# w_phi loaded behind the first v rows, k folds in a row, later output projection steps, in a gated attention and FFN kernel

## The chip, the cores and the metric

One core of one Trainium2 chip runs the whole kernel. The metric is device time in microseconds (us), the median over several executions. Stage times come from one profiled execution of each kernel; there time is counted from the beginning of the span, which is about 1.3 us shorter than the device time. PE is TensorE's matmul pipe, PEld its weight loads, DVE the vector engine, ACT the scalar engine, POOL and SP the other two, and ACTq and SPq the queues on which ACT and SP issue DMAs.

## The reference, cut to what matters

```python
x = A_x                                           # 1 x 2048 x 640, bf16
g = sigmoid((x * gate_w).sum(-1, keepdims=True))
q, k, v = split(x @ wqkv)                         # 32 heads of 20
pq, pk = q @ w_phi, k @ w_phi                     # per head, 20 x 20
phi = lambda p: concat([softmax(p), softmax(-p)]) # for q and k
kv = phi(pk).T @ v ; z = sum(phi(pk))
a = ((phi(pq) @ kv) / (phi(pq) @ z + 1e-6)) @ wo
b = (gelu(x @ w_gate) * (x @ w_up)) @ w_down
return g * a + (1 - g) * b
```

The kernel folds w_phi into the k and q weights once (the "folds": weights times a block diagonal BD made from w_phi), so that it gets pk and pq straight from x.

## The kernel before

First the loads; SP's are issued in this order.

```python
xload("sp", 0); xload("sp", 2)                  # x rows of tiles 0,1 and 2,3; PE transposes them
sc.dma("act", ... wphi_sb <- w_phi ..., reads=["ident"], writes=["wphi"])   # 640 pieces of 40 B
for kt in range(KD):                            # v's weight rows, five loads of 160 KB
    sc.dma("sp", ... w3[:, kt, 0:D] <- wqkv[kt, 2*D:3*D] ..., writes=[("wv", kt)])
sc.dma("act", ... gz <- gate_w ...)
xturn(4, 2)                # x rows of tiles 4,5, transposed by the DMA
wload(self.wkT, D, "wkT")  # k weights, transposed by the DMA
xturn(6, 2)                # x rows of tiles 6,7
wload(self.wqT, 0, "wqT")  # q weights
xturn(8, 4); xturn(12, 4)
... # FFN weights, wo; masks made on POOL
```

Then the start of the attention state. `xt` transposes x on PE, `vs(t, kt)` is one step of v of tile t, `v_early(t, bank)` all of v of a tile, `f(kt, "k"/"q", banks, engine)` a fold with its evacuation to SBUF by DVE ("d") or ACT ("a"), `k_early` the keys of a tile, `pq` a query block, `gram` the update of kv.

```python
for n in (512, 512, 512, 512, 512, 512, 128):   # matmuls of a constant, before x is there
    ... matmul(bank 0, ones, ones)
xt(0, 6, "d"); xt(1, 7, "a"); xt(2, 2, "d"); xt(3, 3, "d")
for t in range(4): vs(t, 0)                     # and so for kt = 1, 2, 3
self.blockdiag()                                # DVE: BD from w_phi and the masks
self.gate_column(6)
... # vs(t, 4) and evacuations
self.v_early(4, 6)
self.v_early(5, 0)
f(0, "k", (2, 3), "d")
f(1, "k", (4, 5), "a")
self.v_early(6, 6)          # needs x of tiles 6,7
f(2, "k", (2, 3), "d")
f(3, "k", (4, 5), "a")
f(4, "k", (0, 1), "d")
self.v_early(7, 6)
self.k_early(0, 2)
f(0, "q", (4, 5), "d")      # needs wqT
f(1, "q", (6, 7), "d")
self.k_early(1, 0)
... # f 2 q, f 3 q, keys 2, f 4 q
self.k_norm(0)              # DVE: sums of the keys' exponentials, reciprocal, scaling
self.k_early(3, 0)
self.k_norm(1)
self.pq(0, 1, 1); self.pq(0, 0, 0); self.pq(0, 3, 3, 0)
self.gram(0)
```

And the order of the output steps of a pair of tiles:

```python
for q in range(2 * nw):
    h, opens = q % nw, q < nw                   # h: a stretch of output columns
    cs = list(range(NFC + 1 if opens else NFC)) + [NFC + 1 + k for k in range(KD)]  # FFN, then wo steps
    for x, c in enumerate(cs): ... # two row halves of PE
```

The softmax here doesn't subtract the row's maximum and nothing guards it: scores larger than these inputs give would overflow.

Of the kernel before, what the change touches and what calls it, by code (L numbers as in the profile page):

```python
# [3 lines left out]
P = 128  # L4
# [103 lines left out]
class _Kernel:  # L108
    S, D, H, DH, F = 2048, 640, 32, 20, 1728
    KD = D // P  # L110
# [4 lines left out]
    NFC = 14  # L115
# [92 lines left out]
    def loads(self):  # L208
        sc, nc = self.sc, self.nc
        D, KD, DH, P_ = self.D, self.KD, self.DH, P  # L210
        w3 = self.wqkv.rearrange("(kt p) n -> p kt n", p=P)

        x4 = self.x[0:self.BT, :].rearrange("(p j) n -> p j n", j=self.TB)

        def xload(q, j):
            sc.dma(q, lambda e: e.dma_start(self.xtok[:, j:j + 2, :], x4[:, j:j + 2, :]),  # L216
                   writes=[("xtok", j), ("xtok", j + 1)])

        def wload(T, c0, key):
            sc.dma("sp", lambda e: e.dma_start_transpose(T[:, :, :], self.wqkv[:, c0:c0 + D]), writes=[key])  # L220

        def xturn(t, n):
            a, z = t * P, (t + n) * P
            sc.dma("sp", lambda e: e.dma_start_transpose(self.xT[:, :, a:z], self.x[a:z, :]),
                   writes=[("xT", k) for k in range(t, t + n)])
        sc.op("pool", lambda e: e.memset(self.gz[:, :], 0.0), writes=["gz"])
        sc.op("act", lambda e: e.activation(self.gtmp[:, 0:1], self.nc.const_aps.tensor(1.0, [P, 1], BF16), AF.Exp),
              writes=["gtmp"])
        sc.op("pool", lambda e: e.memset(self.ident[:, :], 0.0), writes=["ident"])
        sc.op("pool", lambda e: e.affine_select(self.ident[:, :], self.ident[:, :], pattern=[[-1, P]],  # L230
                                                compare_op=ALU.not_equal, fill=1.0, base=0, channel_multiplier=1),
              writes=["ident"])
        xload("sp", 0)
        xload("sp", 2)
        sc.dma("act", lambda e: e.dma_start(
            self.wphi_sb[:, :, :], self.wphi.rearrange("h d f -> (h d) f").rearrange("(i p) f -> p i f", p=P)),
            reads=["ident"], writes=["wphi"])
        for kt in range(KD):
            sc.dma("sp", lambda e: e.dma_start(self.w3[:, kt, 0:D], w3[:, kt, 2 * D:3 * D]), writes=[("wv", kt)])
        sc.dma("act", lambda e: e.dma_start(self.gz[0:KD, :], self.gw.rearrange("(k p) -> k p", p=P)), writes=["gz"])  # L240
        xturn(4, 2)
        wload(self.wkT, D, "wkT")
        xturn(6, 2)
        wload(self.wqT, 0, "wqT")
        xturn(8, 4)
        xturn(12, 4)
        half = 7 * P
        g3 = self.wg.rearrange("(kt p) n -> p kt n", p=P)
        u3 = self.wu.rearrange("(kt p) n -> p kt n", p=P)
        for i, (a, b) in enumerate(((0, half), (half, 13 * P))):  # L250
            sc.dma("sp", lambda e, a=a, b=b: e.dma_start(self.wg_sb[:, :, a:b], g3[:, :, a:b]), writes=[("wg", i)])
            sc.dma("sp", lambda e, a=a, b=b: e.dma_start(self.wu_sb[:, :, a:b], u3[:, :, a:b]), writes=[("wu", i)])
            if i == 0:
                sc.dma("sp", lambda e: e.dma_start(self.wgu_sb[:, :, 0:64], g3[:, :, 13 * P:self.F]), writes=["wgu0"])
                sc.dma("sp", lambda e: e.dma_start(self.wgu_sb[:, :, 64:128], u3[:, :, 13 * P:self.F]), writes=["wgu1"])
        sc.dma("sp", lambda e: e.dma_start(self.wd_sb[:, 0:13, :],
                                           self.wd[0:13 * P, :].rearrange("(c p) n -> p c n", p=P)), writes=["wd"])
        for r in (0, 1):
            sc.dma("sp", lambda e: e.dma_start(self.wd_sb[64 * r:64 * r + 64, 13, :], self.wd[13 * P:self.F, :]),
                   writes=[("wd13", r)])  # L260
        sc.dma("sp", lambda e: e.dma_start(self.wo_sb[:, :, :], self.wo.rearrange("(kt p) n -> p kt n", p=P)),
               writes=["wo"])

        def pool(fn, writes, reads=()):
            sc.op("pool", fn, reads=reads, writes=writes)
        for i in range(KD):
            n = self.HHI[i] - self.HLO[i] + 1
            base = P * i - DH * self.HLO[i]
            m = self.mask[:, i, 0:n]
            pool(lambda e, m=m: e.memset(m, 1.0), [("mask", i)])  # L270
            pool(lambda e, m=m, n=n, base=base: e.affine_select(
                m, m, pattern=[[-DH, n]], compare_op=ALU.is_ge, fill=0.0, base=base, channel_multiplier=1),
                [("mask", i)])
            pool(lambda e, m=m, n=n, base=base: e.affine_select(
                m, m, pattern=[[DH, n]], compare_op=ALU.is_ge, fill=0.0, base=DH - 1 - base, channel_multiplier=-1),
                [("mask", i)])
        for r in (0, 1):
            m = self.hmask[:, r, :, :]
            pool(lambda e, m=m: e.memset(m, 1.0), [("hmask", r)])
            pool(lambda e, m=m, r=r: e.affine_select(  # L280
                m, m, pattern=[[4, KD], [-DH, self.HB]], compare_op=ALU.is_ge, fill=0.0, base=-64 * r,
                channel_multiplier=1), [("hmask", r)])
            pool(lambda e, m=m, r=r: e.affine_select(
                m, m, pattern=[[-4, KD], [DH, self.HB]], compare_op=ALU.is_ge, fill=0.0, base=DH - 1 + 64 * r,
                channel_multiplier=-1), [("hmask", r)])
        for s in range(self.NSV):
            pool(lambda e, s=s: e.memset(self.vaug[:, s, :, DH:self.DA], 1.0), [("vone", s)])
# [133 lines left out]
            reads=[("ps", b0 + 1)], writes=[("gcol", t)])  # L421

    def k_norm(self, t):
        sc = self.sc
        se = t % self.NSE
        H, DH = self.H, self.DH
        sc.op("dve", lambda e: e.tensor_reduce(  # L427
            self.Dk[:, se, 0, :].rearrange("p (s h) -> p s h", h=H),
            self.Ek[:, se, :, :].rearrange("p s (h d) -> p s h d", d=DH), AX.X, ALU.add),
            reads=[("Ek", se, 0), ("Ek", se, 1)], writes=[("Dk", se)])  # L430
        sc.op("dve", lambda e: e.reciprocal(self.Dk[:, se, 1, :], self.Dk[:, se, 0, :]),
              reads=[("Dk", se)], writes=[("Rk", se)])
        for s in (0, 1):
            v = self.Ek[:, se, s, :].rearrange("p (h d) -> p h d", d=DH)
            r = self.Dk[:, se, 1, s * H:(s + 1) * H].unsqueeze(2).to_broadcast([P, H, DH])
            sc.op("dve", lambda e, v=v, r=r: e.tensor_tensor(v, v, r, ALU.mult),  # L436
                  reads=[("Rk", se)], writes=[("Ek", se, s)])
# [97 lines left out]
    def attention_state(self):  # L535
        NT = self.NT
        order = [(b, i) for b in range(self.NB) for i in range(self.KD)]
        sc = self.sc
        ones = self.nc.const_aps.tensor(1.0, [P, 512], BF16)
        for n in (512, 512, 512, 512, 512, 512, 128):  # L540
            sc.op("pe", lambda e: e.matmul(self.bank(0, n), ones[:, 0:P], ones[:, 0:n], start=True, stop=True),
                  writes=[("ps", 0)])
        vs, ve, xt = self.v_step, self.v_first_evac, self.x_transpose
# [18 lines left out]
                ve([0, 1, 2], "a", True)  # L562
        ve([3], "d", True)
        f = self.fold
        self.v_early(4, 6)
        self.v_early(5, 0)
        f(0, "k", (2, 3), "d")
        f(1, "k", (4, 5), "a")
        self.v_early(6, 6)
        f(2, "k", (2, 3), "d")  # L570
        f(3, "k", (4, 5), "a")
        f(4, "k", (0, 1), "d")
        self.v_early(7, 6)
        self.k_early(0, 2)
        f(0, "q", (4, 5), "d")
        f(1, "q", (6, 7), "d")
        self.k_early(1, 0)
        f(2, "q", (4, 5), "d")
        f(3, "q", (6, 7), "d")
        self.k_early(2, 2)  # L580
        f(4, "q", (4, 5), "d")
        self.k_norm(0)
        self.k_early(3, 0)
        self.k_norm(1)
        self.pq(0, 1, 1)
        self.pq(0, 0, 0)
        self.pq(0, 3, 3, 0)
        self.columns = True
        self.gram(0)
        self.k_norm(2)  # L590
# [101 lines left out]
    def down_pair(self, t0, banks, widths):  # L692

        sc = self.sc
        ts = (t0, t0 + 1)
        NFC, KD = self.NFC - 1, self.KD
        nw = len(widths)
# [39 lines left out]
            sc.dma("sp", lambda e: e.dma_start(rows[:, :, c0:c1], self.outsb[:, os_:os_ + 2, c0:c1]),  # L737
                   reads=[("outsb", os_ + j, k) for j in (0, 1) for k in hs], writes=[("out", t0, h)])

        for q in range(2 * nw):  # L740
            h, opens = q % nw, q < nw
            cs = list(range(NFC + 1 if opens else NFC)) + [NFC + 1 + k for k in range(KD)]
            for x, c in enumerate(cs):
                for r in (0, 1):
                    mm(r, r if opens else 1 - r, h, c, opens, x, len(cs))
                if x == len(cs) - 1 and not opens:
                    evac(h)
                yield None

# [94 lines left out]
```

## Time and profile before

| | before |
|---|---|
| device time, median of 3 | 288.31 us (287.94 to 288.32) |
| span of the profiled run | 287.0 us |
| PE busy | 280.9 us, 98% |
| first v step starts | 6.36 us |
| first k fold starts | 14.59 us |
| gram 0 starts | 29.52 us |
| start of the last matmul, last landing | 283.84 and 287.00 us |

From the page of the kernel before: the span, busy times, granted clock by fortieths of the span, and the chain that ended last by engine and by line. L354 is the common projection and gate/up helper.

```profile
span 287.0 us, 7005 instructions
...
PE 280.9 (98%) x3017; PEld 185.7 (65%) x3032; DVE 174.9 (61%) x353; ACT 104.5 (36%) x199; POOL 5.3 (2%) x36
...
PEclk9999999999999999999999999999999999999999
...
PE 96%; DMA 2%; issue 1%; SPq 0%; ACT 0%
PE ps L354 61%; PE ps L713 28%; PE ps L657 2%; PE ps L366 2%; PE ps L452 2%; DMA w<-in_A_wqkv_dram 2%; PE ps L334 1%; SPq L216 0%; ACT outsb L726 0%; PE ps L316 0%
```

PE is busy 98% of the span, and 96% of the last chain is PE. So only PE's idle time or its slow stretches can be won. The waits of PE alone show one in the middle of work (columns: line, what it waited for, total us, times, longest us):

```profile
engine line waited for: us in total, times, longest us
PE ps L366 <- DMA w<-in_A_wqkv_dram: 1.1, 1, 1.1
PE ps L541 <- PEq L829: 0.8, 1, 0.8
```

The timeline of PE gives the moments (start us, us, engine, line, operation, out<-in, shapes, count, and in brackets the idle time before and what ended it):

```profile
3.72 1.53 PE L293 MATMUL ps<-ident,xtok 128*128 128x128 bf16 x20
6.36 4.53 PE L366 MATMUL ps<-w,xT 128*128 128x480 bf16 x32 [1.11 <-DMA w<-in_A_wqkv_dram]
...
14.59 0.79 PE L334 MATMUL ps<-BD,wkT 128*128 128x140 bf16 x12
15.33 1.53 PE L354 MATMUL ps<-w,xT 128*128 128x512 bf16 x10
16.70 1.11 PE L334 MATMUL ps<-BD,wkT 128*128 128x140 bf16 x18
```

The 20 transposes of x (L293) end near 5.25 us. The v steps (L366) then wait 1.11 us for the v weights. After two k folds (L334, 12 matmuls, start 14.59), v 6 starts at 15.33. No wait is noted there, but the trace's record of landings has the x rows of tiles 6 and 7 complete at 15.29 us. Two lines of the same timeline show w_phi's issue, and the block diagonals that need it:

```profile
1.69 0.47 ACTq L235 DMA_DIRECT2D wphi_sb<-in_A_w_phi_dram  x1
...
7.50 1.19 DVE L307 TENSOR_TENSOR BD<-wphi_sb,mask 128x140 bf16<-128x140 bf16 x5 [1.60 <-DMA wphi_sb<-in_A_w_phi_dram]
```

### The profile page before, as it was taken

How to read it: one execution, taken by the hardware profiler on the slowest of the kernel's cores; microseconds unless marked ns; L12 is line 12 of the kernel's file. 1: busy time of each engine (PE TensorE's matmuls, PEld its weight loads, DVE VectorE, ACT ScalarE, POOL GpSimd, SP SyncE). 2: the span in 40 equal slices, each digit the busy share in tenths (PEclk: the TensorE clock that was granted, in tenths of full speed). 3: DMA queues.
4: the chain of work that ended last, by engine and by line, in shares of the span. 5: the costliest groups of instructions: out<-in, count | busy, mean ns of one | idle time of the engine just before them, and what ended most of it. 6: DMA issues, size and time to landing. Idle time of an engine off the chain costs nothing.

```text
span 287.0 us, 7005 instructions
## 1 busy us (share of the span) xinstructions
PE 280.9 (98%) x3017; PEld 185.7 (65%) x3032; DVE 174.9 (61%) x353; ACT 104.5 (36%) x199; POOL 5.3 (2%) x36
## 2 busy tenths in 40 slices
PE   7999999999999999999999999999999999999995
PEld 3576689999994444444444444445777777777785
DVE  1348999999977553567242334225883883883801
ACT  3357887677653222322323223321112112112111
POOL 7000000000000000000000000000000000000000
PEclk9999999999999999999999999999999999999999
DMA  8999996000002000011000000000232343342121
GB/s 224 203 174 248 366 366 192 0 2 2 2 0 48 0 0 0 3 24 23 2 0 0 0 2 0 0 2 0 26 87 74 29 48 99 43 60 82 49 72 48
DMA packets 36937, 18.67 MB, mean 65 GB/s; under 512 B 28970, under 2 KB 36394, under 8 KB 36906
## 3 DMA queue, kind: packets, MB, share of 16 engines
q1 hardware_dynamic: 36240, 18.19, 26.8%
q8 instruction: 24, 0.39, 0.6%
q10 hardware_dynamic: 666, 0.03, 0.2%
q14 instruction: 7, 0.06, 0.1%
HBM read 9.04 MB, written 2.62 MB: 41 GB/s over the span
## 4 chain that ended last, share of the span: by engine, by line
PE 96%; DMA 2%; issue 1%; SPq 0%; ACT 0%
PE ps L354 61%; PE ps L713 28%; PE ps L657 2%; PE ps L366 2%; PE ps L452 2%; DMA w<-in_A_wqkv_dram 2%; PE ps L334 1%; SPq L216 0%; ACT outsb L726 0%; PE ps L316 0%
## 5 line engine op out<-in xcount | busy, mean ns | idle before, releaser
L354 PE MATMUL ps<-xT,wg_sb 128*128 128x512 bf16 (+1 forms) x265 | 63.8, 379 | 0.4 <-issue 0.2
L354 PE MATMUL ps<-xT,wu_sb 128*128 128x512 bf16 (+1 forms) x263 | 63.3, 379 | 0.5 <-DVE hT L631 0.2
L629 ACT ACTIVATE gl<-ps 128x512 bf16<-128x512 f32 x52 | 30.9, 596 | 73.1 <-PE ps L354 68.7
L631 DVE TENSOR_TENSOR hT<-ps,gl 128x512 bf16<-128x512 f32 x39 | 26.7, 690 | 38.3 <-PE ps L354 38.2
L713 PE MATMUL ps<-wd_sb,hT 64*128 64x320 bf16 x648 | 49.4, 296 | 0.0
L354 PEld LDWEIGHTS ps<-xT,wu_sb 128*128 128x128 bf16 (+1 forms) x270 | 26.5, 99 | 29.7 <-DVE hT L631 0.5
L354 PEld LDWEIGHTS ps<-xT,wg_sb 128*128 128x128 bf16 (+1 forms) x270 | 26.2, 99 | 29.0 <-ACT gl L629 0.2
L354 PE MATMUL ps<-w,xT 128*64 128x512 bf16 (+6 forms) x398 | 41.6, 325 | 0.2
L726 ACT ACTIVATE outsb<-ps,Gm 128x320 bf16<-128x320 f32 (+2 forms) x31 | 14.5, 515 | 72.4 <-PE ps L713 72.4
L713 PEld LDWEIGHTS ps<-wd_sb,hT 64*128 64x128 bf16 x648 | 31.0, 94 | 12.2 <-issue 0.4
L354 PEld LDWEIGHTS ps<-w,xT 128*64 128x64 bf16 (+1 forms) x400 | 35.6, 107 | 5.0
L713 PE MATMUL ps<-wo_sb,goT 64*128 64x320 bf16 (+2 forms) x340 | 27.8, 288 | 0.0
L354 PE MATMUL ps<-xT,wq 128*64 128x512 bf16 (+1 forms) x184 | 25.9, 380 | 0.1
L436 DVE TENSOR_TENSOR Ek<-Ek,Dk 128x640 bf16<-128x640 bf16 x32 | 25.0, 822 | 0.6
L684 DVE TENSOR_TENSOR O<-ps,RH 128x640 bf16<-128x640 f32 x32 | 24.8, 816 | 0.0
L427 DVE TENSOR_REDUCE Dk<-Ek 128x64 f32<-128x1280 bf16 x16 | 23.7, 1479 | 0.0
L416 ACT ACTIVATE Ek<-ps 128x640 bf16<-128x640 f32 x32 | 20.7, 703 | 3.5 <-PE ps L354 3.5
L521 ACT ACTIVATE Eq<-ps 128x512 bf16<-128x512 f32 x40 | 21.6, 607 | 0.7 <-PE ps L354 0.4
L631 DVE TENSOR_TENSOR xT<-ps,gl 128x512 bf16<-128x512 f32 x13 | 9.0, 692 | 18.2 <-PE ps L354 18.2
L713 PEld LDWEIGHTS ps<-wo_sb,goT 64*128 64x128 bf16 x340 | 16.0, 94 | 5.4
L354 PEld LDWEIGHTS ps<-xT,wq 128*64 128x64 bf16 (+1 forms) x185 | 15.3, 108 | 2.9
L713 PE MATMUL ps<-wd_sb,xT 64*128 64x320 bf16 (+2 forms) x270 | 16.7, 269 | 0.0
(69 smaller groups left out, 172.9 us busy)
## 6 DMA issues: line engine op xcount, KB each, us to landing
out_dram<-outsb SPq DMA_DIRECT2D x7, 320.0 KB, 2.3
wd_sb<-in_B_w_down_dram SPq DMA_DIRECT2D x1, 2080.0 KB, 12.9
wg_sb<-in_B_w_gate_dram SPq DMA_DIRECT2D x1, 1120.0 KB, 5.8
wu_sb<-in_B_w_up_dram SPq DMA_DIRECT2D x1, 1120.0 KB, 9.5
wg_sb<-in_B_w_gate_dram SPq DMA_DIRECT2D x1, 960.0 KB, 9.6
wu_sb<-in_B_w_up_dram SPq DMA_DIRECT2D x1, 960.0 KB, 10.2
w<-in_A_wqkv_dram SPq DMA_DIRECT2D x5, 160.0 KB, 4.5
wo_sb<-in_A_wo_dram SPq DMA_DIRECT2D x1, 800.0 KB, 9.4
```

Source lines behind the costliest of these rows:

```text
L354: self.sc.op("pe", lambda e: e.matmul(self.ps[a:z, bank * 512 + c0:bank * 512 + c0 + n], lhs[:, a:z], rhs, start=first, stop=fin), reads=r ...
L366: sc.op("pe", lambda e, c0=c0, n=n, bk=bk, col=col: e.matmul(self.bank(bk)[:, col:col + n], self.xT[:, kt, t * P:(t + 1) * P], self.w3[:, ...
L416: self.sc.op("act", lambda e, s=s, scale=scale: e.activation(self.Ek[:, se, s, :], self.ps[:, o:o + self.D], AF.Exp, scale=scale), reads=[ ...
L427: sc.op("dve", lambda e: e.tensor_reduce(self.Dk[:, se, 0, :].rearrange("p (s h) -> p s h", h=H), self.Ek[:, se, :, :].rearrange("p s (h d ...
L436: sc.op("dve", lambda e, v=v, r=r: e.tensor_tensor(v, v, r, ALU.mult), reads=[("Rk", se)], writes=[("Ek", se, s)])
L452: sc.op("pe", lambda e: e.matmul(self.ps[a:a + 64, b * 512 + c:b * 512 + c + 2 * nf], va[:, lo:lo + 64], self.Ek[:, se, :, f0:f0 + nf], st ...
L521: sc.op("act", lambda e, s=s, scale=scale: e.activation(self.Eq[:, s, i, b * self.BT:(b + 1) * self.BT], self.bank(bank), AF.Exp, scale=sc ...
L629: sc.op("act", lambda e: e.activation(self.gl[:, slot, :], self.bank(banks[0]), AF.Gelu_apprx_tanh), reads=[("ps", banks[0])], writes=[("g ...
L631: sc.op("dve", lambda e: e.tensor_tensor(hT, self.bank(banks[1]), self.gl[:, slot, :], ALU.mult), reads=[("ps", banks[1]), ("gl", slot)], ...
L684: dve(lambda e, o=o, f=f, s=s: e.tensor_tensor(o, V[s][:, :, :, 0:DH], f, ALU.mult), rb + [key(6 + s)], [("O", s, sl)], guard=old)
L713: sc.op("pe", lambda e: e.matmul(self.bank(bk, w), lhs, rhs, start=opens and x == 0, stop=end and not opens, skip_group_check=True), reads ...
L726: sc.op("act", lambda e: e.activation(dst, self.bank(bk, w), AF.Copy, scale=g), reads=rd, writes=wr)
```

## The change

The intent: get w_phi's many small pieces out of the way of the v weights, put the work whose inputs land late behind work whose inputs are there, start the DVE sums of keys 0 early, and put the output projection steps of a pair's opening behind all its FFN steps.

```diff
-        sc.dma("act", ... wphi_sb <- wphi ..., reads=["ident"], writes=["wphi"])
         for kt in range(KD):
             sc.dma("sp", ... w3[:, kt, 0:D] ...)
-        sc.dma("act", ... gz <- gw ...)
@@ behind the masks on POOL
+        sc.dma("act", ... wphi_sb <- wphi ..., reads=[("mask", 1)], writes=["wphi"])
+        sc.dma("act", ... gz <- gw ...)
@@ k_norm is split into k_sums and k_scale
@@ attention_state (ve, ke: v_early, k_early)
         f(0, "k", (2, 3), "d")
         f(1, "k", (4, 5), "a")
-        self.v_early(6, 6)
-        f(2, "k", (2, 3), "d")
-        f(3, "k", (4, 5), "a")
-        f(4, "k", (0, 1), "d")
-        self.v_early(7, 6)
-        self.k_early(0, 2)
+        f(2, "k", (6, 7), "d")
+        f(3, "k", (0, 1), "a")
+        f(4, "k", (2, 3), "d")
+        ve(6, 4)
+        ke(0, 6)
+        self.k_sums(0)
+        ve(7, 0)
+        ke(1, 2)
         f(0, "q", (4, 5), "d")
         f(1, "q", (6, 7), "d")
-        self.k_early(1, 0)
+        ke(2, 0)
... (the rest of the q folds and keys in the same manner, on other banks; keys 3 in two
     projections, one ahead of the last q fold and one behind it)
-        self.k_norm(0)
+        self.k_scale(0)
@@ down_pair
-        for q in range(2 * nw): ... FFN steps then wo steps for each h
+        opening: FFN steps of every h, then the wo steps of every h
+        closing: as before
```

More of the change, by code (lines that the diff above doesn't have):

```diff
@@ L234, in loads @@
         xload("sp", 2)
-        sc.dma("act", lambda e: e.dma_start(
-            self.wphi_sb[:, :, :], self.wphi.rearrange("h d f -> (h d) f").rearrange("(i p) f -> p i f", p=P)),
-            reads=["ident"], writes=["wphi"])
         for kt in range(KD):
             sc.dma("sp", lambda e: e.dma_start(self.w3[:, kt, 0:D], w3[:, kt, 2 * D:3 * D]), writes=[("wv", kt)])
-        sc.dma("act", lambda e: e.dma_start(self.gz[0:KD, :], self.gw.rearrange("(k p) -> k p", p=P)), writes=["gz"])
         xturn(4, 2)
@@ L276, in loads @@
                 [("mask", i)])
+        sc.dma("act", lambda e: e.dma_start(
+            self.wphi_sb[:, :, :], self.wphi.rearrange("h d f -> (h d) f").rearrange("(i p) f -> p i f", p=P)),
+            reads=[("mask", 1)], writes=["wphi"])
+        sc.dma("act", lambda e: e.dma_start(self.gz[0:KD, :], self.gw.rearrange("(k p) -> k p", p=P)), writes=["gz"])
         for r in (0, 1):
@@ L423, in k_norm, with k_sums @@
     def k_norm(self, t):
+        self.k_sums(t)
+        self.k_scale(t)
+    def k_sums(self, t):
         sc = self.sc
@@ L430, in k_norm, with k_scale @@
             reads=[("Ek", se, 0), ("Ek", se, 1)], writes=[("Dk", se)])
+    def k_scale(self, t):
+        sc = self.sc
+        se = t % self.NSE
+        H, DH = self.H, self.DH
         sc.op("dve", lambda e: e.reciprocal(self.Dk[:, se, 1, :], self.Dk[:, se, 0, :]),
@@ L564, in attention_state @@
         f = self.fold
-        self.v_early(4, 6)
-        self.v_early(5, 0)
+        ve, ke = self.v_early, self.k_early
+        ve(4, 6)
+        ve(5, 0)
         f(0, "k", (2, 3), "d")
         f(1, "k", (4, 5), "a")
-        self.v_early(6, 6)
-        f(2, "k", (2, 3), "d")
-        f(3, "k", (4, 5), "a")
-        f(4, "k", (0, 1), "d")
-        self.v_early(7, 6)
-        self.k_early(0, 2)
+        f(2, "k", (6, 7), "d")
[6 more added lines that the diff above has]
+        ke(1, 2)
         f(0, "q", (4, 5), "d")
         f(1, "q", (6, 7), "d")
-        self.k_early(1, 0)
+        ke(2, 0)
         f(2, "q", (4, 5), "d")
-        f(3, "q", (6, 7), "d")
-        self.k_early(2, 2)
+        f(3, "q", (2, 3), "d")
+        self.proj(3, 640, 384, 6, 128, ["wk2"])
         f(4, "q", (4, 5), "d")
-        self.k_norm(0)
-        self.k_early(3, 0)
+        self.proj(3, 1024, 257, 7, 0, ["wk2", "wgate"])
+        self.k_evac(3, 6)
+        self.k_scale(0)
         self.k_norm(1)
-        self.pq(0, 1, 1)
-        self.pq(0, 0, 0)
-        self.pq(0, 3, 3, 0)
+        self.pq(0, 1, 1, 0)
+        self.pq(0, 0, 0, 1)
+        self.pq(0, 3, 3, 2)
         self.columns = True
@@ L738, in evac @@
                    reads=[("outsb", os_ + j, k) for j in (0, 1) for k in hs], writes=[("out", t0, h)])
-        for q in range(2 * nw):
-            h, opens = q % nw, q < nw
-            cs = list(range(NFC + 1 if opens else NFC)) + [NFC + 1 + k for k in range(KD)]
-            for x, c in enumerate(cs):
+        wos = [NFC + 1 + k for k in range(KD)]
+        opening = list(range(NFC + 1)) + wos
+        for part in (range(NFC + 1), range(NFC + 1, len(opening))):
+            for h in range(nw):
+                for x in part:
+                    for r in (0, 1):
+                        mm(r, r, h, opening[x], True, x, len(opening))
+                    yield None
+        closing = list(range(NFC)) + wos
+        for h in range(nw):
+            for x, c in enumerate(closing):
                 for r in (0, 1):
-                    mm(r, r if opens else 1 - r, h, c, opens, x, len(cs))
-                if x == len(cs) - 1 and not opens:
+                    mm(r, 1 - r, h, c, False, x, len(closing))
+                if c == closing[-1]:
                     evac(h)
```

## The prediction

> **What bounds the kernel now.** TensorE. The page gives PE 280.9 us busy of a 287.0 us span at full granted clock; the chain that ended last is 96% PE. Windows from 30 us on show PE 5.00 of 5.00 us busy, and the rate is the array's: a gate/up piece of 49 matmuls of 512 columns takes 10.74 us, 219 ns each, against 512/2.4 + 2.5 = 216 ns (the warm spacing in the Trainium skill, TensorE: Matmul & The Clock Gate). So only PE idle time can be won: 0.8 us at launch, 1.1 us before the first v matmul, a few tenths up to 30 us, and 3 us of output tail.
>
> The 1.1 us: by the timeline the transposes of x end on PE near 5.25 us, and the first v matmul starts at 6.36, released by the load of the first v rows. That load was issued at 1.73 and landed at 6.2; the x rows just ahead took 3.0 us. In between, w_phi (640 packets of 40 B, ACT queue, issued at 1.69) is in flight: most of its packets start between 3.9 and 5.0 us, and there the SP queue's rate falls to half (104 KB per quarter microsecond before, 43 to 70 during). I estimate 0.6 to 0.7 us of stolen time. This agrees with the Trainium skill, DMA: Bandwidth & Descriptors, "Queues, rings and completion order": each DMA engine takes turns between queues.
>
> **What the change does.**
> 1. w_phi waits for the second mask (POOL, done at 2.8 us); issued at 2.9 us, its packets start near 5.1. The first v rows should land at 5.0 to 5.4 us. Next limit: the copies of xT (DVE, last ends at 5.90). v steps start near 5.2, the fourth at 6.0. Gain 0.8 to 1.1 us. Later v rows have slack (landings 0.45 us apart, a round of four steps takes 1.08). w_phi lands near 8.7; block diagonals (1.19 us) and gate copy are done near 10.2, before bank 6 is wanted at 11.0.
> 2. The reordering leaves PE's work the same. It keeps the gain: shifted by 1.1 us, v 6 would wait for its x (used at 15.33, just when it landed) and the q folds for wqT (landed about 20.36, used at 20.40). The new order puts both uses back behind the landings. Five folds of 0.32 us outrun their evacuations (0.82 DVE, 0.70 ACT): 0.1 to 0.2 us of wait at the fifth.
> 3. Early sums of keys 0 take 1.48 us from DVE's busy stretch at 25 to 30 us, so gram 0 does not wait. No gain by itself.
> 4. Late output projection steps: between 198 and 284 us PE has no wait. 0, at worst +0.1 us where a closing waits for an opening only five steps old.
>
> **Sum.** -1.1 + 0.15 = about -1.0 us: 287.3 us, 0.35% less. Range 286.8 to 287.9. Faster by over 2%: 1%; within 2%: 98%; slower: 1%.
>
> **What would show it.** First v matmul at 5.1 to 5.5 us; the wait for v rows under 0.3 us; BD starting at 8 to 9.5 us; gram 0 on PE at 28.5 us instead of 29.5; everything after 1.0 us earlier; the stage from first output step to last matmul unchanged (86.2 us).
>
> **What would make it wrong.** v rows late for another cause than w_phi (then no gain); w_phi landing after 10 us, holding DVE and bank 6; wkT landing after 13.5 us; a fold or evacuation wait over 0.2 us.

## The result, and the profile after

| | before | after |
|---|---|---|
| device time, median of 6 | 288.12 us (287.72 to 288.32) | 287.33 us (286.69 to 288.05) |
| ratio | | 0.9976, 95% interval 0.9958 to 0.9995 |
| span of the profiled run | 287.0 | 286.2 |
| first v weights landed | 6.22 | 5.02 |
| first v step, second round of v steps | 6.36, 7.45 | 5.78, 7.09 |
| full clock granted from | 4.26 | 6.22 |
| x of tiles 6,7 landed; v 6 starts | 15.29; 15.33 | 14.85; 16.24 |
| gram 0 | 29.52 | 29.13 |
| start of the last matmul; last landing | 283.84; 287.00 | 283.49; 286.18 |

A ratio here is the mean time of one kernel's fast runs over that of the other's of the same rounds, so it is not quite the ratio of the medians. 0.9976 of 288 us is 0.7 us less. The predicted 287.3 is met as a number, though it was 1.0 us less than a kernel before of 288.3.

The same parts of the page after:

```profile
span 286.2 us, 7006 instructions
...
PE 281.8 (98%) x3017; PEld 186.7 (65%) x3032; DVE 174.9 (61%) x353; ACT 104.5 (37%) x199; POOL 5.3 (2%) x36
...
PEclk9999999999999999999999999999999999999999
...
PE 98%; issue 0%; ACT 0%
PE ps L354 61%; PE ps L726 28%; PE ps L670 2%; PE ps L366 2%; PE ps L461 2%; PE ps L334 1%; PE ps L550 1%; PE ps L293 1%; ACT outsb L739 0%; PE ps L316 0%
```

PE's waits after: the wait for the v weights is gone, and nothing over 0.2 us stands in the middle of work.

```profile
PE ps L550 <- PEq L849: 0.8, 1, 0.8
PE ps L354 <- DVE hT L644: 0.2, 1, 0.2
PE ps L354 <- issue: 0.2, 1, 0.2
```

The timeline of PE after:

```profile
3.67 2.31 PE L293 MATMUL ps<-ident,xtok 128*128 128x128 bf16 x20
5.78 4.76 PE L366 MATMUL ps<-w,xT 128*128 128x480 bf16 x32
...
14.23 1.96 PE L334 MATMUL ps<-BD,wkT 128*128 128x140 bf16 x30
16.24 5.39 PE L354 MATMUL ps<-w,xT 128*128 128x512 bf16 x39
```

The v steps start without a wait, but only 0.58 us earlier, because the same 20 transposes took 2.31 us instead of 1.53. Since v steps also ran slowly at first (4.76 us instead of 4.53), the second round is only 0.36 us earlier. The k folds now stand in a row (30 matmuls), and v 6 starts 2.01 us after the first of them instead of 0.74. w_phi was issued 1.17 us later, yet BD was made no later than before:

```profile
2.86 0.43 ACTq L273 DMA_DIRECT2D wphi_sb<-in_A_w_phi_dram  x1
...
7.36 1.18 DVE L307 TENSOR_TENSOR BD<-wphi_sb,mask 128x140 bf16<-128x140 bf16 x5 [0.85 <-DMA wphi_sb<-in_A_w_phi_dram]
```

Lastly the tail. The three last output issues on the SP queue and ACT's last evacuation, before and after:

```profile
281.72 4.00 SPq L737 DMA_DIRECT2D out_dram<-outsb  x3
...
284.12 0.37 ACT L726 ACTIVATE outsb<-ps,Gm 128x128 bf16<-128x128 f32 x1 [0.53 <-PE ps L713]
```

```profile
281.37 3.53 SPq L750 DMA_DIRECT2D out_dram<-outsb  x3
...
283.77 0.37 ACT L739 ACTIVATE outsb<-ps,Gm 128x128 bf16<-128x128 f32 x1 [0.53 <-PE ps L726]
```

Before, the issues end at 285.72 us, 1.23 us after that evacuation (284.12 + 0.37). After, they end at 284.90, 0.76 us after it. Of the 0.82 us between the two last landings, 0.35 us was already there at the last matmul and 0.47 us came from this tail. So the pair of traces gives the right sum with parts that the prediction did not have, and the experiments had to find which of them belong to the change.

### The profile page after: what moved, and what is told of

Its sections match the earlier page's. It is cut to its first block, busy times and chain, and to the rows that moved or that the text cites. A ratio compares the mean times of both kernels' runs of the same rounds, so it can differ in the third digit from the quotient of the medians.

```text
span 286.2 us, 7006 instructions
## 1 busy us (share of the span) xinstructions
PE 281.8 (98%) x3017; PEld 186.7 (65%) x3032; DVE 174.9 (61%) x353; ACT 104.5 (37%) x199; POOL 5.3 (2%) x36
## 4 chain that ended last, share of the span: by engine, by line
PE 98%; issue 0%; ACT 0%
PE ps L354 61%; PE ps L726 28%; PE ps L670 2%; PE ps L366 2%; PE ps L461 2%; PE ps L334 1%; PE ps L550 1%; PE ps L293 1%; ACT outsb L739 0%; PE ps L316 0%
## 5 line engine op out<-in xcount | busy, mean ns | idle before, releaser
L726 PE MATMUL ps<-wd_sb,hT 64*128 64x320 bf16 x648 | 48.5, 296 | 0.0
L726 PE MATMUL ps<-wo_sb,goT 64*128 64x320 bf16 (+2 forms) x340 | 26.5, 288 | 0.0
L726 PE MATMUL ps<-wd_sb,xT 64*128 64x320 bf16 (+2 forms) x270 | 16.0, 269 | 0.0
```

What stands on the lines that cost most here:

```text
L726: sc.op("pe", lambda e: e.matmul(self.bank(bk, w), lhs, rhs, start=opens and x == 0, stop=end and not opens, skip_group_check=True), reads ...
```

## The experiments

The theories:

- A, clock: with the wait for the v weights gone, PE is busy from the first transpose on, and the gain depends on when the full clock is granted.
- B, data: the start is fixed by landings.
- C, reordering: the new order, and not w_phi, is what gains.
- D, late steps: the late output steps shorten the tail.

E to H came later, after the first traces:

- E: what the change wins is v 6's wait for its x rows. F: it is the rest of the order.
- G: an earlier first transpose is won in full.
- H: the landing of the x rows of tiles 6 and 7 is not what the old order loses by.

All timed runs are 6 executions each; "before" in a ratio is the kernel before in the same rounds.

### The changed kernel again (e4_after_again)

No edit.

> The changed kernel itself, once more. Theory A (clock): since the wait for the v rows is gone, TensorE is busy without a break from the first transposes of x (3.7 us), and what is left of the gain depends on when the full clock is granted (4.26 us in the trace of before, 6.22 us in that of after[...]). The instant will be another one, between 4.2 and 7.7 us, and the second round of v steps will start at about 6.3 us if it is 4.3, 7.1 if it is 6.2, 7.7 if it is 7.6. Timed runs scatter over about 1 us. Rival B (data): the v steps are held by the x rows or v rows; then the second round starts at 7.1 us again whatever the clock, and the runs scatter no more than those of the kernel before (0.6 us). Ratio 0.9965 to 0.999 by both.

Measured: 287.68 us (286.97 to 289.30), ratio 0.9979 (0.9953 to 1.0005). Full clock at 6.66 us, first transpose at 3.93, second round at 7.43. This supports A: 20 transposes of 128 columns and 4 v steps of 640 are 5,120 columns. The single transposes of 128 columns start about 107 ns apart before the full clock and 56 after it (the Trainium skill, TensorE: Matmul & The Clock Gate, "Wait — 56ns, not 53.3ns?", has 106.7 and 55.6), which is 1.2 and close to 2.4 columns a nanosecond. With these rates the second round should start at 7.43 us, and it did. For the trace after (3.67, 6.22) the same sum gives 7.08, measured 7.09, and it comes within 0.02 us in all ten of the fourteen traces where the full clock came at 5.89 us or later. B expected 7.1 again and fell. The tail from the last matmul's start to the last landing was 2.56 us.

### w_phi's move alone (e1_wphi_only)

```diff
 (kernel before)
-  w_phi and gate weights loaded ahead of and behind the v weights
+  both issued behind the second mask, as in the change
```

> The kernel before with w_phi and the gate weights moved as in the change, nothing else. Theory A: the first v rows land at about 5.0 us and the whole gain at the start is there (second round of v steps 0.35 to 1.1 us earlier, by the clock); later it is kept if the clock came late, and partly lost at v 6 (its x lands near 14.9 us) and at the q folds (their weights land near 20.2 us) if the clock came early: 0.2 to 0.6 us less in sum. Time 0.3 to 0.8 us under before. Rival C: the reordering is what gains; then this is equal to before within 0.2 us.

Measured: 287.90 us, ratio 0.9984 (0.9964 to 1.0005): not told apart from before. As it stands, 0.5 us less is what theory A expected and not what rival C did, but the interval holds both. The profiled run had the earliest clock of all, 3.57 us. The second round started at 6.70 us, 0.39 us ahead of the trace after, but gram 0 at 29.19, 0.06 behind it. The lead was lost where theory A said it would be, at v 6 (PE's timeline):

```profile
3.91 1.55 PE L293 MATMUL ps<-ident,xtok 128*128 128x128 bf16 x20 [0.25 <-DMA xtok<-in_A_x_dram]
5.62 4.53 PE L366 MATMUL ps<-w,xT 128*128 128x480 bf16 x32 [0.16 <-DMA w<-in_A_wqkv_dram]
...
13.84 0.79 PE L334 MATMUL ps<-BD,wkT 128*128 128x140 bf16 x12
14.98 1.53 PE L354 MATMUL ps<-w,xT 128*128 128x512 bf16 x10 [0.35 <-DMA xT<-in_A_x_dram]
```

v 6 started 1.14 us after the first fold. Without a wait it is 0.63 (see e7_before_again). The x rows of tiles 6 and 7 landed at 14.94 us.

### The change with w_phi in its old place (e2_wphi_old)

```diff
 (changed kernel)
+  w_phi and gate weights loaded where the kernel before loads them
-  their loads behind the second mask
```

> The changed kernel with w_phi and the gate weights loaded where they were. Theory A: the v rows land at 6.2 us again, the second round of v steps starts at 7.4 us as before, the reordered part costs 0.1 to 0.2 us for the wait of the fifth k fold; time 0.0 to 0.3 us over before. Rival C (the reordering gains): 0.3 us or more under before.

Measured: 287.43 us (287.28 to 287.85), ratio 0.9965 (0.9947 to 0.9984). Theory A said 0.0 to 0.3 us over before; it was 1.0 us under, and the interval leaves out 1. Rival C was right: no loss is seen when w_phi goes back. The first v weights landed at 5.68 us, not 6.2, and PE did not wait for them.

### The change with the old output order (e3_no_late)

```diff
 (changed kernel)
-        opening: FFN steps of every h, then wo steps of every h
+        for q in range(2 * nw): ... as in the kernel before
```

> The changed kernel with the output projection steps in their old order. Theory A: the same as the changed kernel within 0.2 us, and the stage from the first output step to the last matmul lasts 85.5 us in both. Rival D: the 0.47 us by which the tail after the last matmul was shorter in the trace of the changed kernel (2.43 us against 2.94) comes from the late steps; then the tail is 2.9 us here and the time 0.4 to 0.5 us over the changed kernel.

Measured: 287.65 us, ratio 0.9968 (0.9948 to 0.9988). The tail was 3.11 us, as rival D said, but the time was not over that of the changed kernel (0.9976 and 0.9979). The stage from the first output step to the last matmul was 85.95 us here and after; the "85.5" in the expectation was a slip.

### The kernel before against itself (e7_before_again)

> The kernel before against itself: what the scatter of start, clock and tail is worth. Ratio 1.000 within 0.002. Theory A (clock and landing): the full clock comes between 3.5 and 6.9 us, the first v rows land between 5.6 and 6.3 us, the second round of v steps starts 7.0 to 7.5 us, gram 0 22.0 to 22.2 us after it. Rival D (late steps shorten the tail): from the start of the last matmul to the last landing 2.9 to 3.2 us; else between 2.5 and 3.2.

Measured: 288.33 us (287.30 to 288.61), ratio 1.0007 (0.9986 to 1.0027). The profiled run was the fastest of the six. PE's timeline:

```profile
3.86 2.32 PE L293 MATMUL ps<-ident,xtok 128*128 128x128 bf16 x20 [0.19 <-DMA xtok<-in_A_x_dram]
5.96 4.64 PE L366 MATMUL ps<-w,xT 128*128 128x480 bf16 x32
...
14.30 0.79 PE L334 MATMUL ps<-BD,wkT 128*128 128x140 bf16 x12
14.93 1.52 PE L354 MATMUL ps<-w,xT 128*128 128x512 bf16 x10
```

With w_phi in its early place the first v weights landed at 5.29 us, 0.93 us earlier than in the trace of before and below the 5.6 to 6.3 expected, and there is no wait ahead of the v steps. The trace of the DMA packets shows the same fall of the SP queue's rate while w_phi's packets run (40 to 59 KB per quarter microsecond from 4.25 to 5.0 us, about 100 from 2.75 to 3.75), so the fall is there with the early landing too. Instead the clock was late (6.18), and the transposes took 2.32 us, as in the trace after. So the 1.1 us wait on which the prediction rested was a matter of that one execution. x of tiles 6 and 7 landed early here, at 14.71 us, so v 6 followed the first fold after 0.63 us with no wait. The tail was 2.60 us with the old output order.

### The late output steps alone (e8_late_only)

```diff
 (kernel before)
-        for q in range(2 * nw): ... FFN steps then wo steps for each h
+        opening: FFN steps of every h, then the wo steps of every h
```

> The kernel before with the late output projection steps alone. Theory A: no effect, ratio 1.000 within 0.002, from the first output step to the last matmul 85.9 us as in all runs so far. Rival D: the tail from the start of the last matmul to the last landing is 2.55 to 2.7 us (the three runs with late steps had 2.56, 2.69, 2.70; the three without 2.75, 3.11, 3.16), the last output issue takes 0.6 to 0.75 us instead of 0.8 to 1.2, and the time is 0.3 to 0.5 us under before.

Measured: 288.05 us, ratio 0.9997 (0.9978 to 1.0016), tail 2.80 us. D's shorter tail is not there. Over all fourteen traces the tail is 2.56 to 3.01 us (mean 2.76 of seven) with late steps and 2.60 to 3.16 (mean 2.85 of seven) without.

### w_phi loaded twice (e9_wphi_twice)

```diff
 (kernel before)
   sc.dma("act", ... wphi_sb <- wphi ..., reads=["ident"], writes=["wphi"])
+  sc.dma("act", ... wphi_x  <- wphi ..., reads=["ident"], writes=["wphix"])   # read by nobody
```

> The kernel before with w_phi loaded twice in its early place, the second time into a tile that nothing reads. If w_phi's small packets hold up the v rows by about 0.5 us a load: first v rows land at 6.5 us or later (single: 6.2 and 5.7), second round of v steps at 7.7 us or later, time 0.3 to 0.5 us over before. If they cost nothing: 5.7 to 6.2 us and the time of before.

Measured: 288.24 us, ratio 1.0006 (0.9984 to 1.0027). The first v weights landed at 5.16 us with twice the small pieces in their way; only three runs had them earlier. One trace alone can't refute that w_phi holds them up by 0.5 us, but all fourteen speak against it: with w_phi early the landings are 5.16 to 5.68 us in six of seven traces and 6.22 in the first (mean 5.47), with w_phi moved 5.02 to 5.58 (mean of seven 5.28). The trace showed something else:

```profile
3.80 1.72 PE L297 MATMUL ps<-ident,xtok 128*128 128x128 bf16 x20
5.35 4.67 PE L370 MATMUL ps<-w,xT 128*128 128x480 bf16 x32
...
13.72 0.79 PE L338 MATMUL ps<-BD,wkT 128*128 128x140 bf16 x12
16.35 1.53 PE L358 MATMUL ps<-w,xT 128*128 128x512 bf16 x10 [1.84 <-DMA xT<-in_A_x_dram]
```

The clock came early (4.74) and the first fold started at 13.72, earlier than in any other run. Then PE stood for 1.84 us at v 6, because its x landed at 16.31 us; gram 0 came at 30.54. In the old order an early start is worth nothing when these rows land late.

### No matmuls ahead of x (e5_after_no_warm)

```diff
 (changed kernel)
-        for n in (512, 512, 512, 512, 512, 512, 128):
-            ... matmul(bank 0, ones, ones)
```

> The changed kernel without the seven matmuls of a constant that keep TensorE busy before x arrives. Theory A (the clock's instant is a cost on the critical path): the full clock comes 2.9 us later on average, between 6.4 and 10.3 us; matmuls before it run at half the rate, the second round of v steps starts at 7.5 to 8.2 us, and the time is 0.5 to 1.7 us over the changed kernel. Rival B (data bound start): second round at 7.1 us and the same time within 0.2 us.

Measured: 289.05 us (287.70 to 289.96), ratio 1.0028 (1.0001 to 1.0054), against 0.9976 and 0.9979 for the changed kernel: about 1.4 us more, as A said. Part of this is not in the span: two of the six runs (289.24 and 288.86 us) have spans of only 286.4 and 286.6, which stays unexplained. By mean spans the kernel is 0.3 us over before (287.12 against 286.84), and the changed kernel in e4_after_again 0.7 under (286.62 against 287.33), so about 1.0 us remains. The profiled run was a lucky one (287.81): full clock at 6.77 us, second round at 7.38, a little under the expected 7.5.

```profile
3.72 2.31 PE L293 MATMUL ps<-ident,xtok 128*128 128x128 bf16 x20 [3.72 <-DMA xtok<-in_A_x_dram]
5.82 5.00 PE L366 MATMUL ps<-w,xT 128*128 128x480 bf16 x32
```

### One piece of the reordering (e11_v6_behind_folds)

```diff
 (kernel before)
-        self.v_early(6, 6)
-        f(2, "k", (2, 3), "d")
-        f(3, "k", (4, 5), "a")
-        f(4, "k", (0, 1), "d")
+        f(2, "k", (6, 7), "d")
+        f(3, "k", (0, 1), "a")
+        f(4, "k", (2, 3), "d")
+        self.v_early(6, 4)
```

> The kernel before with one piece of the reordering: the five k folds in a row, then v 6 and v 7; all else as before, w_phi too. Theory E (what the change wins is v 6's wait for its x rows): in the kernels with the old order the stretch from the second round of v steps to gram 0 was 21.94, 22.07, 22.23, 22.49, 23.96 us, longer by what the landing of x 6 (14.7 to 16.3 us) exceeds the time v 6 is wanted; in those with the new order 22.04 or 22.05 always. Here v 6 is wanted 1.75 us after the first fold, so not before 15.4 us: the stretch is 22.0 to 22.3 us (the q folds are wanted as early as before, at 20.0 us or later, and can wait 0.2 us for their weights), and the time is 0.3 to 0.9 us under before. Rival F (the rest of the order, keys ahead of the q folds and the early sums, is what wins): as before within 0.2 us.

Measured: 287.83 us, ratio 0.9991 (0.9970 to 1.0012), not told apart from before. The point, 0.3 us under, is the least that E expected and close to F (within 0.2 us), so F is not ruled out. v 6 started 1.79 us after the first fold with no wait. The stretch from the second round to gram 0 was nonetheless 22.46 us, since the wait had moved to the q folds, which the old order wants just as early:

```profile
20.71 0.80 PE L334 MATMUL ps<-BD,wqT 128*128 128x140 bf16 x12 [0.21 <-DMA wqT<-in_A_wqkv_dram]
```

The q weights landed at 20.66 us in this run, and the fold started at 20.71. PE's matmuls are 0.48 us apart there. This suggests that the piece that puts keys 1 ahead of the q folds is needed too; it was not tried alone. How much each piece is worth on average was not settled.

### x rows split over two queues (e12_after_x_split)

```diff
 (changed kernel)
-        xload("sp", 0); xload("sp", 2)            # two tiles a load
+        for j in range(4): xload(("sp", "act")[j % 2], j)   # one tile a load
-        for n in (512, 512, 512, 512, 512, 512, 128):
+        for n in (512, 512, 512, 512, 512, 256):
```

> The changed kernel with the first four x rows in four loads of one tile each, alternating between the SP and the ACT queue, and 384 columns fewer of the constant matmuls, so that the first transpose can start earlier. Theory G (TensorE is busy from the first transpose on, so an earlier start is won in full): first transpose at 3.2 to 3.5 us instead of 3.7 to 3.9, the second round of v steps 0.2 to 0.4 us earlier for the same instant of the clock, gram 0 22.04 us after it, time 0.2 to 0.4 us under the changed kernel (0.9 to 1.2 under before). If the loads land no earlier: no change.

Measured: 287.61 us (287.46 to 287.88), ratio 0.9984 (0.9962 to 1.0006). It did not do what it was made for: the first load, now half as large, landed at 3.77 us, inside the 3.62 to 4.04 us of the other runs, and the first transpose started at 3.81. So G was not tested. x of tiles 6 and 7 landed at 16.20 us, and the new order waited only 0.09 us for it. The stretch to gram 0 was 0.32 us over the usual 22.04; the rest of that was not followed up.

### The x rows of tiles 6 and 7 made late (e14_before_x6_late, e15_after_x6_late)

```diff
 (kernel before; changed kernel)
   wload(self.wkT, D, "wkT")
+  sc.dma("sp", ... extra <- 320 KB of x ...)     # read by nobody
   xturn(6, 2)
```

> The kernel before with 320 KB more, read by nobody, loaded on the SP queue just ahead of the x rows of tiles 6 and 7; by the rate of that queue they land 0.8 to 1.0 us later, at 15.6 to 16.8 us. Theory E (the old order makes TensorE wait at v 6 for these rows): v 6 starts when they land, the stretch from the second round of v steps to gram 0 is 22.7 to 23.8 us, and the time is 0.6 to 1.0 us over before. Rival H (the landing is not what the old order loses by): stretch 21.9 to 22.2 us, time as before within 0.2 us.

> The changed kernel with the same extra load. Theory E: v 6 is wanted about 1.1 us later in the new order (1.75 us after the first fold instead of 0.63), so most of the delay is absorbed: stretch 22.04 to 22.5 us, time 0.0 to 0.4 us over the changed kernel, and 0.8 to 1.5 us under the kernel before with the extra load. The q folds' weights land 0.8 to 1.0 us later too, near 21.0 us, still ahead of 21.5 us, when they are wanted. Rival H: both kernels move by the same amount.

Measured: 289.95 us (287.90 to 291.15), ratio 1.0035 (0.9993 to 1.0077), with the old order; 288.08 us (287.43 to 288.93), ratio 0.9970 (0.9939 to 1.0002), with the new one. The means of six are 289.83 and 288.13 us, but that gap can't be given to the rows. Three of the six old-order runs (290.80 to 291.15), and two of the eleven runs of the kernel before beside them (290.74 and 290.94), have a mean granted clock of 0.994, where every other timed run has 0.999 or 1.000. By an estimate from these figures (0.006 of 289 us) the clock alone takes 1.7 us of such a run. Without these five the means are 288.66 (old order, three runs), 288.61 (kernel before, nine) and 288.13 us (new order, six): the old order then lost nothing by the extra load, and the new one is 0.5 us below it. None of the five was traced, so whether the late rows or something else brought the lower clock stays open. Neither E nor H is decided here. The profiled run of the old order was the fastest of its six; the rows landed at 15.32 us there, and the stretch was 22.14 us, not the 22.7 to 23.8 expected. So its trace shows no loss. The trace of the new order shows a wait that even the new order does not cover; its stretch was 23.57 us, over the 22.5 that E allowed:

```profile
13.86 1.95 PE L337 MATMUL ps<-BD,wkT 128*128 128x140 bf16 x30
17.17 5.61 PE L357 MATMUL ps<-w,xT 128*128 128x512 bf16 x40 [1.36 <-DMA xT<-in_A_x_dram]
```

The rows landed at 17.13 us and the clock was early (4.93), so v 6 had to wait 1.36 us. The new order absorbs 1.38 us more than the old one (2.01 less 0.63); it does not remove the dependence.

### All runs side by side

"Wait at v 6" is the start of v 6 minus the start of the first fold, less 0.63 us in the old order and 2.01 in the new (0.63 is the time in e7_before_again, and 2.01 the time of five new-order runs in which the rows had landed before v 6 was wanted). It is 0 where that gives 0.03 or less. In e11_v6_behind_folds the sum is not formed. The ratio of e14 includes the runs at the lower clock.

| run | order | full clock | v weights | 2nd round | x 6,7 landed | wait at v 6 | gram 0 | 2nd round to gram 0 | ratio |
|---|---|---|---|---|---|---|---|---|---|
| before | old | 4.26 | 6.22 | 7.45 | 15.29 | 0.12 | 29.52 | 22.07 | |
| e7 before again | old | 6.18 | 5.29 | 7.16 | 14.71 | 0 | 29.10 | 21.94 | 1.0007 |
| e8 late only | old | 6.38 | 5.16 | 7.30 | 15.30 | 0.28 | 29.53 | 22.23 | 0.9997 |
| e1 w_phi only | old | 3.57 | 5.48 | 6.70 | 14.94 | 0.51 | 29.19 | 22.49 | 0.9984 |
| e9 w_phi twice | old | 4.74 | 5.16 | 6.58 | 16.31 | 2.00 | 30.54 | 23.96 | 1.0006 |
| e14 x 6 late | old | 6.51 | 5.28 | 7.44 | 15.32 | 0.16 | 29.58 | 22.14 | 1.0035 |
| e11 v 6 only | piece | 6.49 | 5.51 | 7.33 | 15.08 | - | 29.79 | 22.46 | 0.9991 |
| e2 w_phi old | new | 6.47 | 5.68 | 7.31 | 14.98 | 0 | 29.36 | 22.04 | 0.9965 |
| e3 no late | new | 6.23 | 5.58 | 7.18 | 15.81 | 0 | 29.22 | 22.04 | 0.9968 |
| after | new | 6.22 | 5.02 | 7.09 | 14.85 | 0 | 29.13 | 22.04 | 0.9976 |
| e4 after again | new | 6.66 | 5.38 | 7.43 | 15.01 | 0 | 29.48 | 22.04 | 0.9979 |
| e5 no warm | new | 6.77 | 5.12 | 7.38 | 15.50 | 0 | 29.42 | 22.04 | 1.0028 |
| e12 x split | new | 5.89 | 5.30 | 7.00 | 16.20 | 0.09 | 29.36 | 22.36 | 0.9984 |
| e15 x 6 late | new | 4.93 | 5.07 | 6.72 | 17.13 | 1.30 | 30.29 | 23.57 | 0.9970 |

After gram 0 nothing differs: from there to the last matmul it is 254.31 to 254.36 us in thirteen of the runs and 254.18 in e12.

## Why the prediction was right or wrong

The number was right by luck: the main step that led to it was wrong, and another step was given no gain although it is where the gain is.

1. "TensorE bounds the kernel": right. The constant 254.3 us from gram 0 to the last matmul shows that the change won nothing there.
2. "I estimate 0.6 to 0.7 us of stolen time" for w_phi: this step failed. The one trace showed a late landing of the v weights and w_phi's packets ahead of it, and the prediction made the second the cause of the first. With w_phi in the same place the weights landed at 5.29 us (e7), and with it loaded twice at 5.16 (e9). With w_phi moved they landed at 5.02 to 5.58. PE's wait for them was 1.1 us in one trace of fourteen, 0.16 in another, and none in the rest. The fall of the SP queue's rate is real, but it is there in e7 too, with the landing 0.93 us earlier: it did not decide the landing. Nor is all of it w_phi's. From 4.0 to 5.0 us the queue moved 224 KB in the trace before and 330 KB in the trace after, where w_phi's packets come later; by an estimate from these two figures (106 KB fewer, at 330 KB a microsecond) w_phi took about 0.3 us, not 0.6 to 0.7, and the mean landings (5.47 and 5.28 us) differ by still less. Why they landed at 6.22 in the first trace stays open.
3. "Gain 0.8 to 1.1 us, first v matmul at 5.1 to 5.5 us": it was 5.78 us, and gram 0 came at 29.13 instead of 28.5. The copies of xT were taken as the next limit. In the runs with a late clock the limit was the transposes themselves, which run at half rate until the full clock comes. The copies were the limit only where it came early: in e9 and e15 the weight loads of the v steps stood 0.30 us for ACT's copy. In the trace before, that clock came at 4.26 us, and the prediction took it for a fixed property.
4. "The reordering leaves PE's work the same. It keeps the gain": its mechanism was right and even named the two loads, x of tiles 6 and 7 and wqT. Its place in the sum was wrong. The waits at v 6 are a cost of the kernel before, 0 to 0.5 us in four traces and 2.0 in a fifth. The trace before had them hidden: the late v weights had pushed v 6 back to the moment when its rows landed. The four timed kernels with the whole new order and the old dummy matmuls and x loads have ratios of 0.9965 to 0.9979, with w_phi early or late and with late steps or without. The kernels with the old order and without extra loads of x have 0.9984 to 1.0007. These ratios are not all independent: e2, e3, e4 and e1 share one set of runs of the kernel before, whose mean of 288.57 us is above the 288.06 to 288.08 of the earlier and later rounds at full clock. Against e1, the old-order kernel of the same round (mean 287.95), the new-order ones are 0.06 to 0.45 us less (287.89, 287.57, 287.50).
5. "0.1 to 0.2 us of wait at the fifth" fold: right in size. In the trace after, the fifth fold starts 0.46 us after the fourth, where the first ones are 0.31 apart. Over the whole start the new order takes 22.04 us from the second round to gram 0 where nothing lands late; the old order takes 21.94 (e7). That 0.10 us is the price of the new order.
6. "Early sums of keys 0: gram 0 does not wait. No gain by itself": nothing contradicts it (stretches of 22.04 us); the sums were not tried alone.
7. "Late output projection steps: 0": right (0.9997 alone; 85.95 us in the output stage).
8. "BD starting at 8 to 9.5 us": it started at 7.36. w_phi landed 4.5 us after its issue instead of 5.8.

So the cause that the runs support is this. The new order gains: the gain is there without w_phi's move (e2) and without the late steps (e3), though the order was never run with both of them left out. Why it gains is shown only in part. The traces show that it lets the x rows of tiles 6 and 7 land 1.38 us later without a wait, at the price of 0.1 us: in e3 they landed at 15.81 us, 0.86 us after the old order would have wanted them (14.32 plus 0.63), and PE did not wait. It also puts the q folds 7.24 us behind the first k fold (trace after) instead of 5.73 (e7), which covers a late landing of the q weights such as e11 waited for. That it also lets an early clock count is argued, not shown in a trace (e15 had the early clock, but late rows); it fits that the lowest of all times of the changed kernel, 286.69 us, lies under all of the kernel before (287.06 at the lowest).

What stays open is whether these waits are the whole gain. The waits at v 6 average 0.23 us over the first four old-order runs of the table and 0.58 with e9. Taking the landings of all twelve traces without the extra load of x, an estimate of the old order's wait is 0.48 us on average and of the new order's 0.06; less the 0.1 us of its price, the new order should win about 0.3 us. The ratios of the new order speak for 0.6 to 1.0 us, the comparison with e1 in the same round for 0.06 to 0.45. The direct test, e14 and e15, decided nothing. Most timed runs were not traced. A small gain by w_phi's move (0.9984, interval to 1.0005) is neither shown nor excluded. No experiment gave a kernel that is clearly faster than the changed one.

## What to carry to other kernels

When the expected effect is under a microsecond, take the trace of the same kernel twice before explaining a wait: here the largest wait of the first trace was not there in the second, and a cost that the first hid stood in others. Put work whose inputs land late, and at scattered times, behind work whose inputs are there, even where one trace shows the input arriving just in time. "Just in time" in one trace can mean a wait in others, as at v 6 here. When removing a wait at the start of a kernel, count what PE does up to that point at half rate, since the full clock may not have come yet.

## What the Trainium skill lacked or had wrong

- TensorE: Matmul & The Clock Gate, "What's actually happening", says that the window by which the clock is granted is free-running, so that the moment varies by 500 ns either way. The moment varies, but by far more: with the same matmuls of a constant from 0.84 us on, the full clock came between 3.57 and 6.66 us. In ten traces the second round of v steps followed it, from 7.00 to 7.44 us. The page's spacings for 128 columns ("Wait — 56ns, not 53.3ns?"), 106.7 and 55.6 ns, agree: 20 transposes took 2.31 us where all were ahead of the full clock and 1.53 us where it came in their midst, counting the last one's latency.
- The same section calls for a busy window of about 3.4 us sustained. In e1_wphi_only PE began at 0.8 us and had the full clock at 3.57, after 2.7 us; in e5_after_no_warm it began at 3.72 and had it at 6.77, after 3.05 us. In these two runs less than 3.4 us was enough.
- DMA: Bandwidth & Descriptors, "Queues, rings and completion order", says that each DMA engine takes turns between queues. The prediction named this beside a delay that it estimated from the trace, and the runs did not show the delay (5.16 us with twice the small pieces, 6.22 with one set). The page has no figure for how much the landing of one and the same load scatters: here the first v weights, issued at 1.73 us within 0.01 in all runs looked at, landed from 5.02 to 6.22 us over all runs, and the x rows of tiles 6 and 7 from 14.71 to 16.31 us in the runs without the extra load of x.
- The same page, "Anatomy of one DMA — SWDGE (gpsimd) path", gives a fixed part of about 2 us and a part by size (fitted for another issuing path). Halving the first x load brought it no earlier (3.77 us; 3.62 to 4.04 in the others). Two such half loads were in flight together there, so this is no test of the page's sum; what sets the landing of this load was not found.
